# Attention and gate in one kernel: the value products in two row halves with a PSUM bank each, and six shared banks instead of seven

## The chip, the cores and the metric

The kernel runs on one core of a Trainium2 chip. The metric is the time of one execution on the device in microseconds. The core's engines work in parallel, each on its own queue of instructions: TensorE multiplies (PE in the profile; its weight loads are listed apart as PEld), VectorE (DVE) and ScalarE (ACT) do elementwise work and reductions, GpSimd (POOL) works between SBUF tiles, SyncE (SP) starts the transfers. Products land in PSUM, eight banks of 128 partitions by 512 f32, and are read from there by DVE and ACT.

## The reference

With `x` of 2048 rows and 640 columns, 32 heads of 20 columns and a hidden width of 1536 (`xn` is `x` normalised by row):

```python
q, k, v = split_heads(xn @ wqkv)
p = softmax(q @ k.T * 20 ** -0.5)            # for each head, 2048 x 2048
s = merge_heads(p @ v) @ wo
g = silu(relu(xn @ w1) @ w2)
out = x + s * g
```

The change touches `p @ v` and the division by the softmax's sum that follows it.

## The kernel before

Heads are worked on in 8 groups of 4 (`NG`), the queries in 4 chunks of 512 (`NC`, `CW`), the keys in 16 tiles of 128 (`NT`). One *step* is a group, a chunk and a key tile: 8 x 4 x 16 = 512 steps (`STEPS`).

For every group and chunk the kernel does three things with the scores:

- It finds the largest score of each query. `mx_unit` (lines 617 to 638) multiplies queries by keys in f16 into a PSUM bank (line 629), and DVE takes the maximum of the bank (line 633). `highest` and `rows` (lines 640 to 691) gather the maxima, turn them with one transpose into a PSUM bank (line 661), and send them into two extra rows of the packed queries.
- It computes the scores again the other way round, keys by queries, with the maximum subtracted by the extra rows. `st_unit` (lines 719 to 746) does the product (line 732), and ACT writes the exponentials in f32 into a tile `pt` (line 736). Four such products, one for each head, make the weights of one step; three `pt` tiles are in use in turn (`PTS`).
- It weighs the values. `weigh` (lines 764 to 776) multiplies, for each of the four heads, the 128 keys of the step (f32, 21 columns: 20 of the head and a one, which sums the weights) by the 512 weights, and adds the product into the bank `pv`. Head `h` writes partitions 32h to 32h + 20, so four products with a stationary operand of 128 rows and 21 columns stand side by side in the array. After 16 steps `normalise` (lines 780 to 819) copies `pv` into an SBUF tile `sb` of 128 x 512, by ACT or DVE, whichever the plan has free earlier (lines 783 to 788). Later `rest` turns `sb` with four transposes into one shared bank (line 794), and DVE divides (lines 797 and 800).

The score products have 60 or 62 rows. They are always issued in pairs (`pair`, lines 645 to 656), one on rows 0 to 63 of the array and one on rows 64 to 127, each into a bank of its own. `KINDS` (line 1227) lists what may be paired: two scores for the maximum, two for the exponentials, or one of each.

All other large products are *fill*: the projections of queries, keys and values, the gate's two layers and the output projection. `products` (lines 298 to 320) cuts each of them into row halves as well: two results, two banks, and each half of the 128 rows goes to one of the two tiles of 64 rows, first straight, then crossed (line 314). Without score work to go with it, `whole` (lines 322 to 330) uses all 128 rows (line 328). A fill product holds its two banks from its first matmul until ACT or DVE has read them.

PSUM holds `pv` (line 173) and 7 shared banks (`BANKS`, line 174). Scores, fill products and the transposes take shared banks with `take` (lines 182 to 187), which gives the one that comes free first; a pair or a fill product needs two (`take_two`, and `soonest(2)` in `choose`).

The order of all engines' instructions is made when the program is built, by a planner (`Plan`, lines 81 to 154) and a loop over it (lines 1252 to 1301). It keeps a clock for each engine and estimated costs in ns (lines 52 to 78: `PAIR` 220 for a pair, `PV` 850 for a step of values, `SWITCH` 100 between kinds of matmul, `EXP` 585, `RED` 605). At each turn it issues a pair if banks are free and ACT or DVE will soon run out of work; else one or two steps of values, if their weights are ready (`pv_count`, lines 748 to 762; the first step of a chunk also waits for `pv_free`, the time at which the copy of the last chunk is done); else small work such as the transposes; else a fill product, at a pace that spreads the fill over the attention (`pace`, lines 1245 to 1250). Each engine then runs its own queue in that order and waits on semaphores for what it reads or overwrites.

Of the kernel before, what the change touches and what calls it, by code (L numbers as in the profile page):

```python
# [11 lines left out]
F32 = mybir.dt.float32  # L12
# [5 lines left out]
P = 128  # L18
# [3 lines left out]
DH = 20  # L22
# [3 lines left out]
NT = S // P  # L26
CW = 512
# [5 lines left out]
NP = H // 2  # L33
RING = 4
PTS = 3
BANKS = 7
STEPS = NG * NC * NT
INF = float("inf")

# [118 lines left out]
def attention_gate(ctx: ExitStack, tc: tile.TileContext, x, wqkv, wo, w1, w2, out):  # L158
    nc = tc.nc
    ctx.enter_context(tc.manual_schedule())  # L160
    plan = Plan()
# [7 lines left out]
    psum = ctx.enter_context(tc.tile_pool(name="psum", bufs=1, space=bass.MemoryType.PSUM))  # L169

    pv = psum.tile([P, CW], F32, name="pv")
    banks = [psum.tile([P, CW], F32, name=f"ps{i}") for i in range(BANKS)]
    bank_free = [0.0] * BANKS
    behind = [0] * BANKS

# [4 lines left out]
    def take():  # L182

        i = min(range(BANKS), key=lambda i: bank_free[i])
        ready = bank_free[i]
        bank_free[i] = INF
        return i, ready
# [5 lines left out]
    nc.vector.memset(ones_row, 1.0)  # L193
    root = const.tile([1, 1], F32, name="root")
    nc.scalar.activation(root, ones_row[:, 0:1], AF.Sqrt)
    nc.vector.memset(pv, 0.0)

    qk_d = {w: dram.tile([D, 3, S], F16, name=f"{w}_d") for w in "qk"}
    h_d = {part: dram.tile([DFF, S], F16, name=f"h{part}_d") for part in "hl"}
# [23 lines left out]
    def soon(ready, cost, fn):  # L223
        small.append((ready, cost, fn))
# [329 lines left out]
    va = [vap.tile([P, NT, H // 2, DH + 1], F32, name=f"va{n}") for n in range(2)]  # L554
# [142 lines left out]
    pv_free = [0.0]  # L697
# [8 lines left out]
    def where(step):  # L706
        return step // (NC * NT), step // NT % NC, step % NT
# [56 lines left out]
    def weigh():  # L764
        step = pv_done[0]
        g, c, k = where(step)
        pv_done[0] += 1
        pt = pts.pop(step)
        plan.seen = max(plan.seen, st_issued.pop(step))
        got = plan.pe("P", PV, max(p_ready.pop(step), pv_free[0] if k == 0 else 0))  # L770
        for h in range(4):
            nc.tensor.matmul(pv[32 * h:32 * h + DH + 1, :], va[g // 4][:, k, 4 * (g % 4) + h, :], pt[:, h, :],  # L772
                             start=(k == 0), stop=(k == NT - 1))
        pt_free[step] = plan.t + BACK
        if k == NT - 1:
            normalise(g, c, got)
# [3 lines left out]
    def normalise(g, c, got):  # L780
        epool = pools["ep"]
        sb = epool.tile([P, CW], F32, name=f"pvs{g}{c}", tag="pvs")
        if plan.free["act"] < plan.free["dve"]:
            nc.scalar.copy(sb, pv)
            pv_free[0] = plan.op("act", 600, got)
        else:
            nc.vector.tensor_copy(sb, pv)
            pv_free[0] = plan.op("dve", 690, got)

        def rest():  # L790
            b, free = take()
            tp = banks[b].rearrange("p (i h d) -> p i h d", i=TPC, h=4)
            for i in range(TPC):
                nc.tensor.transpose(banks[b][:, i * P:(i + 1) * P], sb[:, i * P:(i + 1) * P], ident)
            got = plan.pe("F", 4 * TURN, free)
            rl = epool.tile([P, TPC, 4], F32, name=f"rl{g}{c}", tag="rl")
            nc.vector.reciprocal(rl, tp[:, :, :, DH])
            plan.op("dve", 250, got)
            dst = on if g + 1 < NG else on[:, :, P - 4 * DH:]
            nc.vector.tensor_mul(dst.rearrange("p i (h d) -> p i h d", d=DH), tp[:, :, :, 0:DH],  # L800
                                 rl[:, :, :, None].to_broadcast([P, TPC, 4, DH]))
            bank_free[b] = done = plan.op("dve", 490)
            if g + 1 < NG:
                def go():
                    rows = o_d[c * CW:(c + 1) * CW, :].rearrange("(i p) e -> p i e", p=P)
                    nc.sync.dma_start(rows[:, :, 4 * DH * g:4 * DH * (g + 1)], on)
                    o_stored[g, c] = plan.arrival(4 * P * 4 * 4 * DH)

                plan.at(done, go)
            else:  # L810
                first.append(out_rest(c, on, done))

        if g + 1 < NG:
            on = epool.tile([P, TPC, P], F32, name=f"on{g}{c}", tag="on", bufs=NC)[:, :, 0:4 * DH]
        else:
            on = epool.tile([P, TPC, P], F32, name=f"on{g}{c}", tag="on", bufs=NC)
            nc.sync.dma_start(on[:, :, 0:P - 4 * DH],
                              o_d[c * CW:(c + 1) * CW, KL * P:D - 4 * DH].rearrange("(i p) e -> p i e", p=P))
        soon(pv_free[0], 4 * TURN, rest)
# [235 lines left out]
    def out_rest(c, on, ready):  # L1055

        yield from when(lambda: pre_done[0] >= (c + 1) * TPC)
        tail, wot, cs_o, pre = (out_state[n] for n in ("tail", "wo", "scale", "pre"))
        gts = []
        for i in range(TPC):  # L1060
            t = c * TPC + i
            gts.append(tail.tile([P, D], F32, name=f"gr{t}", tag="gr", bufs=6))
            landed = load(gts[i], g_d[t * P:(t + 1) * P, :], 4 * P * D)
        o, ready = yield from transposed(f"r{c}", on, TPC, ready, "r")
        for i in range(TPC):
            t = c * TPC + i
            gt = gts[i]
            ot = o[0][:, i:i + 1, :], o[1][:, i:i + 1, :]
            ws = [w[:, KL:KD, :] for w in wot]
            bs, free = take_two()  # L1070
            got = yield from whole([banks[b][:, 0:HD] for b in bs],
                                      [terms(ot, ws, 1, slice(0, P), ns) for ns in halves], max(free, ready))
            for n, (b, ns) in enumerate(zip(bs, halves)):
                ps = banks[b][:, 0:HD]
                nc.vector.scalar_tensor_tensor(gt[:, ns], ps, cs_o, gt[:, ns], op0=ALU.mult, op1=ALU.mult)  # L1075
                bank_free[b] = done = plan.op("dve", 550, max(got, landed))
                if n and c + 1 == NC:
                    nc.vector.tensor_add(gt[:, ns], gt[:, ns], pre[:, t, ns])  # L1078
                    done = plan.op("dve", 500, done)
                else:  # L1080
                    nc.gpsimd.tensor_add(gt[:, ns], gt[:, ns], pre[:, t, ns])
                    done = plan.op("pool", 880, done)
            plan.at(done, lambda t=t, gt=gt: nc.sync.dma_start(out[t * P:(t + 1) * P, :], gt))
# [168 lines left out]
    while True:  # L1252
        plan.due()
        t = plan.t
# [11 lines left out]
        if n and (coming == INF or min(plan.free["act"], plan.free["dve"]) - t > STOCK or plan.mode != "A"):  # L1266
            for _ in range(n):
                weigh()
            log.append((t, f"pv{n}"))
            continue  # L1270
# [22 lines left out]
        if pv_done[0] * 4 + 4 <= st_done[0]:  # L1293
            g, c, k = where(pv_done[0])
# [32 lines left out]
```

## Time and profile before

| | |
|---|---|
| time, median of 2 runs | 1789.01 us (1787.75 to 1790.27) |
| the profiled execution: its time | 1788.3 us |
| the profiled execution: its span, first to last instruction | 1786.5 us |
| mean granted TensorE clock | 0.992 of full speed |
| idle PE waiting for GpSimd at the start (line 418, longest single wait of PE) | 14.3 us |
| normalise's copies | 23 on ACT, 9 on DVE |
| first and last value product | 125.7 and 1769.8 us |

The profile is one execution, recorded by the hardware. Its rows are groups of instructions: source line, engine, operation, what it writes and reads (buffer numbers left out, so `ps` is any of the shared banks), the shape, how many, then busy time in us, the mean duration of one in ns, and the time that the engine sat idle just before them, with what ended it. For a matmul the shape begins with the rows and columns of the stationary operand: 62*128 is 62 rows and 128 columns. An f32 matmul appears as two, one for each pass over its operand, so line 772 has 4096 rows in the trace for 2048 in the program. Matmuls are pipelined: one of 512 columns is listed with 378 ns while the next starts about 220 ns after it, so busy times of PE overlap and a busy PE is not a PE at its peak. In rows of the order of time the first two numbers are the start and the length in us, and x8 means that eight instructions of one kind follow each other there.

### The profile page before, as it was taken

The numbers are of one execution on the slowest core, as the hardware profiler recorded it, in microseconds if no ns is written. First come the engines' busy times: TensorE is split into PE (matmuls) and PEld (weight loads), VectorE is DVE, ScalarE is ACT, GpSimd is POOL, SyncE is SP. The second block draws the span as 40 slices with busy tenths as digits, with TensorE's granted clock in tenths as the row PEclk, the third lists the DMA queues.
The fourth block names the chain that finished last, engine by engine and source line by source line (L and its number), as shares of the span: only waits on it lengthen the run. The fifth ranks groups of instructions, "written<-read, shape, count | busy, mean of one in ns | idle before, by whom it ended". The sixth has DMA issues, their size and how long they took to land. (4 is left out here: it accounts for less than half of the span.)

```text
span 1786.5 us, 36686 instructions
## 1 busy us (share of the span) xinstructions
PE 1734.0 (97%) x14887; PEld 723.6 (41%) x14887; DVE 1451.6 (81%) x2512; ACT 1390.6 (78%) x2338; POOL 315.9 (18%) x338
## 2 busy tenths in 40 slices
PE   4999999999999999999999989999999999999998
PEld 3443334444332333444433324444444444344332
DVE  7699988888888888888888878888888888887522
ACT  3537788888888888887887868888788878887785
POOL 1631200002111455322221103000000000012221
PEclk8999999999999999999999999999999999999998
DMA  6324311201115332311112071131013100323332
GB/s 240 102 62 125 99 33 35 49 20 37 58 41 162 96 93 89 107 51 43 45 39 73 29 216 42 55 92 56 13 55 92 55 9 20 109 87 124 102 100 74
DMA packets 133995, 135.30 MB, mean 76 GB/s; under 512 B 26640, under 2 KB 110480, under 8 KB 133824
## 3 DMA queue, kind: packets, MB, share of 16 engines
q1 hardware_dynamic: 133248, 131.63, 24.4%
q8 instruction: 116, 1.90, 0.4%
q10 hardware_dynamic: 576, 1.31, 0.2%
q14 instruction: 55, 0.45, 0.1%
HBM read 85.32 MB, written 47.58 MB: 74 GB/s over the span
## 5 line engine op out<-in xcount | busy, mean ns | idle before, releaser
L736 ACT ACTIVATE pt<-ps,cexp 128x512 f32<-128x512 f32 x2048 | 1249.4, 689 | 293.0 <-PE ps L732 244.8
L633 DVE TENSOR_REDUCE m<-ps 128x1 f32<-128x512 f32 x2048 | 1274.4, 684 | 211.0 <-PE ps L629 204.6
L629 PE MATMUL ps<-kp,qp 60*128 60x512 f16 x2048 | 585.6, 378 | 5.3 <-ACT pt L736 3.7
L732 PE MATMUL ps<-qp,kp 62*128 62x512 f16 x2048 | 579.4, 379 | 9.3 <-DVE m L633 4.7
L772 PE MATMUL pv<-pt,va 128*21 128x512 f32 x4096 | 523.0, 600 | 0.0
L732 PEld LDWEIGHTS <-kp 62*128 62x128 f16 x2048 | 147.3, 93 | 332.2 <-issue 289.6
L629 PEld LDWEIGHTS <-qp 60*128 60x128 f16 x2048 | 150.1, 93 | 117.3 <-issue 84.7
L772 PEld LDWEIGHTS pv<-pt,va 128*21 128x21 f32 x4096 | 88.4, 100 | 237.3 <-issue 226.4
L1048 POOL TENSOR_TENSOR pre<-pre,go 128x320 f32<-128x320 f32 x32 | 27.0, 864 | 596.3 <-DVE go L1046 596.3
L314 PE MATMUL ps<-w2th,hh 64*128 64x320 f16 x768 | 126.5, 296 | 0.1
L314 PE MATMUL ps<-w2th,hl 64*128 64x320 f16 x768 | 126.0, 295 | 0.0
L314 PE MATMUL ps<-w2tl,hh 64*128 64x320 f16 x768 | 125.6, 295 | 0.0
L314 PEld LDWEIGHTS <-hh 64*128 64x128 f16 x1536 | 88.2, 94 | 51.2 <-issue 10.5
L314 PE MATMUL ps<-xt_hi,1h 64*128 64x512 f16 x480 | 102.7, 376 | 0.0
L314 PE MATMUL ps<-xt_lo,1h 64*128 64x512 f16 x480 | 102.1, 375 | 0.0
L314 PE MATMUL ps<-xt_hi,1l 64*128 64x512 f16 x480 | 100.3, 375 | 0.5 <-POOL 1l L287 0.5
L314 PEld LDWEIGHTS <-1h 64*128 64x128 f16 x960 | 58.7, 94 | 53.0 <-issue 18.7
L896 POOL CAST hh<-hr 128x512 f16<-128x512 f32 x48 | 29.3, 610 | 287.2 <-ACT hr L894 258.5
L482 POOL TENSOR_TENSOR loq<-rq,hiq 128x512 f16<-128x512 f32 x16 | 18.5, 1159 | 260.2 <-ACT rq L480 260.2
L314 PE MATMUL ps<-xt_hi,qh 64*128 64x512 f16 x150 | 56.4, 376 | 0.0
L314 PE MATMUL ps<-xt_lo,qh 64*128 64x512 f16 x150 | 56.4, 376 | 0.0
L898 POOL TENSOR_TENSOR hl<-hr,hh 128x512 f16<-128x512 f32 x48 | 55.7, 1160 | 3.8
(219 smaller groups left out, 1521.7 us busy)
## 6 DMA issues: line engine op xcount, KB each, us to landing
kp<-k_d SPq DMA_DIRECT2D x28, 240.0 KB
qp<-q_d SPq DMA_DIRECT2D x28, 240.0 KB
hh_d<-hh SPq DMA_DIRECT2D x48, 128.0 KB
hl_d<-hl SPq DMA_DIRECT2D x48, 128.0 KB
hh<-hh_d SPq DMA_DIRECT2D x8, 768.0 KB
hl<-hl_d SPq DMA_DIRECT2D x8, 768.0 KB
q_d<-hiq SPq DMA_DIRECT2D x20, 256.0 KB
k_d<-hik SPq DMA_DIRECT2D x20, 256.0 KB
```

The source lines that it names most:

```text
L314: nc.tensor.matmul(ps[which], a[rows], b[rows], start=(i == 0 and not second), stop=(i == n - 1 and bool(second)))
L482: nc.gpsimd.tensor_sub(lo, r, hi)
L629: nc.tensor.matmul(banks[b], qp[p % RING][r, t:t + P], kp[p % RING][r, kc * CW:(kc + 1) * CW], start=True, stop=True)
L633: nc.vector.tensor_reduce(m4[:, 2 * pr + j, qt, kc:kc + 1], banks[b], axis=AX.X, op=ALU.max)
L732: nc.tensor.matmul(banks[b], kp[p % RING][r, k * P:(k + 1) * P], qp[p % RING][r, c * CW:(c + 1) * CW], start=True, stop=True)
L736: exps[step, u] = nc.scalar.activation(pt[:, u, :], banks[b], AF.Exp, scale=cexp).ins
L772: nc.tensor.matmul(pv[32 * h:32 * h + DH + 1, :], va[g // 4][:, k, 4 * (g % 4) + h, :], pt[:, h, :], start=(k == 0), stop=(k == NT - 1))
L896: nc.gpsimd.tensor_copy(hi, r)
L898: nc.gpsimd.tensor_sub(lo, r, hi)
L1048: nc.gpsimd.tensor_add(pre[:, t, ns], pre[:, t, ns], gts[t][:, ns])
```

## The change

The values of a step are multiplied in two halves of 64 keys. There are two value banks, `pv[0]` for keys 0 to 63 of every tile and `pv[1]` for keys 64 to 127, so each head's product of 128 rows becomes two of 64 rows, both of 512 columns, with 21 columns of stationary operand as before. When a chunk is done, ACT copies the first bank into `sb` and DVE adds the second to it; there is no choice of engine any more, and `pv_free` is set after the add. With two of the eight PSUM banks for values, six are shared. The planner's costs for a step of values (`PV`) and its kinds of matmul stay as they are.

```diff
-BANKS = 7
+BANKS = 6
...
-    pv = psum.tile([P, CW], F32, name="pv")
+    pv = [psum.tile([P, CW], F32, name=f"pv{i}") for i in range(2)]
...
-    nc.vector.memset(pv, 0.0)
+    for t in pv:
+        nc.vector.memset(t, 0.0)
...
         got = plan.pe("P", PV, max(p_ready.pop(step), pv_free[0] if k == 0 else 0))
         for h in range(4):
-            nc.tensor.matmul(pv[32 * h:32 * h + DH + 1, :], va[g // 4][:, k, 4 * (g % 4) + h, :], pt[:, h, :],
-                             start=(k == 0), stop=(k == NT - 1))
+            for half in range(2):
+                rows = slice(half * P // 2, (half + 1) * P // 2)
+                nc.tensor.matmul(pv[half][32 * h:32 * h + DH + 1, :], va[g // 4][rows, k, 4 * (g % 4) + h, :],
+                                 pt[rows, h, :], start=(k == 0), stop=(k == NT - 1))
...
         sb = epool.tile([P, CW], F32, name=f"pvs{g}{c}", tag="pvs")
-        if plan.free["act"] < plan.free["dve"]:
-            nc.scalar.copy(sb, pv)
-            pv_free[0] = plan.op("act", 600, got)
-        else:
-            nc.vector.tensor_copy(sb, pv)
-            pv_free[0] = plan.op("dve", 690, got)
+        nc.scalar.copy(sb, pv[0])
+        done = plan.op("act", 600, got)
+        nc.vector.tensor_add(sb, sb, pv[1])
+        pv_free[0] = plan.op("dve", 690, done)
```

## The prediction

> **What bounds the kernel now.** I read the page's head first, then a table by stage, then the page's costliest groups, and last the order of time on TensorE around the values (line 772).
>
> ```profile
> span 1786.5 us, 36686 instructions
> PE 1734.0 (97%) x14887; PEld 723.6 (41%) x14887; DVE 1451.6 (81%) x2512; ACT 1390.6 (78%) x2338; POOL 315.9 (18%) x338
> ...
> 0.00:126.00 126.00, 100.76 (x574) 51.91 (x578) 97.09 (x208) 51.70 (x92) 43.97 (x49) 0.96 0.42 141
> 126.00:1750.00 1624.00, 1605.09 (x14147) 661.69 (x14143) 1343.54 (x2285) 1320.23 (x2217) 265.10 (x282) 1.00 0.24 71
> 1750.00:1786.00 36.00, 28.19 (x172) 10.04 (x172) 10.94 (x20) 18.69 (x32) 6.86 (x8) 0.87 0.11 42
> ```
>
> The columns of the table are stretch, length, then busy time of PE, PEld, DVE, ACT and POOL, the granted clock, DMA. In the long middle stage PE is busy 1605 of 1624 us at the full clock, DVE 83%, ACT 81%. So time is PE's: a change pays or costs what it takes off or puts on PE there, and the other two have some 280 and 300 us to give.
>
> ```profile
> L736 ACT ACTIVATE pt<-ps,cexp 128x512 f32<-128x512 f32 x2048 | 1249.4, 689 | 293.0 <-PE ps L732 244.8
> L633 DVE TENSOR_REDUCE m<-ps 128x1 f32<-128x512 f32 x2048 | 1274.4, 684 | 211.0 <-PE ps L629 204.6
> L629 PE MATMUL ps<-kp,qp 60*128 60x512 f16 x2048 | 585.6, 378 | 5.3 <-ACT pt L736 3.7
> L772 PE MATMUL pv<-pt,va 128*21 128x512 f32 x4096 | 523.0, 600 | 0.0
> ```
>
> But a busy PE is not a streaming PE. The values are the only large work that leaves the array's 64-row form (60*128, 62*128 and 64*128 in the rows, two tiles side by side) for another: 128*21, four heads side by side. What a visit to that form costs is in the order of time:
>
> ```profile
> 901.52 0.38 PE L314 MATMUL ps<-xt_hi,1l 64*128 64x512 f16 x2
> 901.74 0.38 PE L732 MATMUL ps<-qp,kp 62*128 62x512 f16 x2
> 902.05 1.06 PE L772 MATMUL pv<-pt,va 128*21 128x512 f32 x8
> 903.04 0.39 PE L629 MATMUL ps<-kp,qp 60*128 60x512 f16 x2
> ...
> 1131.77 1.92 PE L772 MATMUL pv<-pt,va 128*21 128x512 f32 x16
> 1133.61 0.39 PE L732 MATMUL ps<-qp,kp 62*128 62x512 f16 x2
> ```
>
> Pairs inside the 64-row form start 0.22 us apart (901.52 to 901.74). The last pair before the values holds the array 0.31 us, 0.09 more. One step of values (x8: each f32 product is two passes, for four heads) takes 0.99 us until the next pair starts, two steps (x16) 1.84. So a step more is 0.85, a pass 0.43, and 0.99 - 0.85 leaves about 0.13 per visit besides the streaming. With the 0.09 ahead, a visit has 0.22 us that is not streaming.
>
> ```profile
> 125.69 1.31 PE L772 MATMUL pv<-pt,va 128*21 128x512 f32 x8
> ...
> 1766.28 4.15 PE L772 MATMUL pv<-pt,va 128*21 128x512 f32 x16
> ```
>
> Between these two, the first and the last, I count 378 visits: 244 of x8 and 134 of x16 (244 + 268 = 512 steps). 378 x 0.22 = 83 us. That is all the change could win on PE, and the question is whether 64-row values (64*21) still leave the form of the scores (62*128).
>
> **The change part by part.**
>
> *Values in halves.* The nearest row is a place where only the width changes:
>
> ```profile
> 1689.99 0.30 PE L328 MATMUL ps<-wo_h,olr 128*128 128x320 f16 x1
> 1690.12 0.30 PE L328 MATMUL ps<-wo_h,ohr 128*128 128x320 f16 x1
> 1690.35 1.06 PE L772 MATMUL pv<-pt,va 128*21 128x512 f32 x8
> ```
>
> Here both sides use 128 rows. The L328 products run 0.13 to 0.14 us apart, the values come 0.23 after the last: 0.095 us lost, as much as the 0.09 where rows and width change together. Equal rows buy nothing as long as the width goes from 128 to 32. After the change rows are equal and the width still goes from 128 to 32, so I take the price of a visit's two ends as unchanged. Its bounds: all of both ends won (0.09 + 0.095 a visit, 70 us), or nothing; I take nothing, since the row with the same single difference says so. By the Trainium skill (TensorEngine Tiling (Array Packing), Key Properties) another tiling mode drains the array and another tile of the same mode does not; as it lists 64x128 and 64x32 apart, its sum would be the same, and the L328 row, where only the width changes, agrees with 0.095 us.
>
> Each step now issues 16 instead of 8 matmuls, and as many weight loads. A half needs as many columns as a whole (512), so a pass stays 0.43 us if all eight tiles run side by side. What grows is the staggered start:
>
> ```profile
> 902.04:902.05 0.01, 0.00 (x1) 1.00 0.00 0
> 902.05:902.06 0.01, 0.01 (x2) 1.00 0.00 0
> 902.06:902.07 0.01, 0.01 (x4) 1.00 0.00 0
> ```
>
> Counts of L772 in 10 ns stretches: one tile has begun in the first, four in the third, so three more starts take about 0.02 us, 0.007 each. Four more tiles: 0.027 us a visit, x 378 = 10 us, on the path, since the next pair needs the whole array. Bounds: 0 (stagger hidden in the 0.13) and, should the whole 0.13 less the 0.095 of the exit scale with the tiles, another 0.035, 13 us. I take 10, as it is counted. By the Trainium skill (TensorE: Matmul & The Clock Gate, Measured speedup vs the span model) one more tile costs about 4 ns; by that page the term would be an estimated 6 us and the sum 4 us lower; the 7 ns of this trace stand.
>
> *Normalise.* One copy, by whichever engine is freer, becomes ACT copy, then DVE add, 32 times.
>
> ```profile
> L784 ACT COPY pvs<-pv x23: 585/585/647, 172.3 to 1678.7; 128x512 f32<-128x512 f32 x23
> L787 DVE COPY pvs<-pv x9: 668/692/693, 287.0 to 1770.5; 128x512 f32<-128x512 f32 x9
> L196 DVE MEMSET pv<- x1: 485/485/485, 1.1 to 1.1; 128x512 f32 x1
> ...
>   PEld pv L772: 2.2, 7
> ```
>
> ACT gets 9 copies more (9 x 0.585 = 5 us); DVE gets 32 adds for 9 copies. No add of this shape is in the trace, I price it as the DVE copy, 0.69: 23 x 0.69 = 16 us. Both lie in the idle time named above. If that cover were gone, 16 us of DVE would be the price. The new wait: the add stands in DVE's queue until ACT's copy is done, so the reduces (L633) behind it wait, up to 32 x 0.59 = 19 us of DVE, and the banks those reduces free come later to PE; fill products (L314) stand in for that. And the two value banks come free 0.7 us later per chunk. Today PE lost 2.2 us to that release in 32 chunks. Bounds: 0, if the next chunk's values come later anyway, and 32 x 0.7 = 22 us if nothing else could run. I take 2, near the row.
>
> The last chunk has no cover:
>
> ```profile
> 1770.47 0.69 DVE L787 COPY pvs<-pv 128x512 f32<-128x512 f32 x1 [6.01 <-PE pv L772]
> 1771.22 0.66 PE L794 MATMUL ps<-ident,pvs 128*128 128x128 f32 x4 [0.79 <-DVE pvs L787]
> ```
>
> PE waits for this copy at the end of the kernel; copy and add in a row make it 0.59 longer: +0.6 us. The second memset (0.49 us at 1.1 us) is long done when the first values start at 125.69: nothing, at most 0.5.
>
> *Six shared banks.* A pair takes two, a running fill product two. 7 = fill + two pairs + one odd bank; 6 = fill + two pairs. What used the odd one are single-bank jobs and a pair that starts when the banks of another come free one by one.
>
> ```profile
> L661 PE MATMUL ps<-ident,m x32: 275/277/383, 112.0 to 1673.5; 128*16 128x128 f32 x32
> L794 PE MATMUL ps<-ident,pvs x128: 272/273/333, 173.3 to 1771.6; 128*128 128x128 f32 x128
> L1011 PE MATMUL ps<-ident,ot x64: 272/273/331, 1543.2 to 1742.2; 128*128 128x128 f32 x64
> L1011 PE MATMUL ps<-ident,on x16: 272/328/422, 1626.4 to 1773.4; 128*128 128x128 f32 x16
> ...
> PE ps L732 <- DVE m L633: 4.7, 7, 2.3
> PE ps L629 <- ACT pt L736: 3.7, 19, 0.3
> ```
>
> That is 32 + 128/4 + 80/4 = 84 jobs. Each now keeps a pair from being in flight, and ACT and DVE run dry for about one operation, 0.7 us (L736, L633): up to 84 x 0.7 = 59 us of theirs. PE's own waits for banks are some 8 us today (the two rows above), because a fill product or values fill the hole; the order is planned anew with six. Bounds for PE: 0 and 59; I take 5, near the waits of today. A new order can also have more or fewer visits, 0.22 us each; I have no row for that.
>
> *Sum.* 1788.3 us is the profiled execution's own time (its span of 1786.5 and 1.8 around it), 0.7 below the median of 1789.0. 1788.3 + 10 (stagger) + 2 (release of the value banks) + 0.6 (end) + 5 (banks) = 1806 us, 1.0% above the median.
>
> **The rivals.**
>
> *The ends of a visit vanish* (faster). If the array only empties when its row grouping changes, 64-row values follow 62-row scores as one pair follows another, and 378 x (0.09 + 0.095) = 70 us go: 1736 us. For it: pairs of 60, 62 and 64 rows follow each other without loss. Against: L328 to L772, the same rows and still 0.095 lost. The other engines would allow it (DVE busy 1452 + 16).
>
> *The halves do not run side by side* (slower). No row shows eight tiles at once. If the second half's first pass queues behind the first half's second, each visit lasts a pass longer: 378 x 0.43 = 163, 1969 us. If every step is doubled, 512 x 0.85 = 435, 2241 us. Against: two row tiles run at once in every pair (x2 lasts 0.38, one matmul 378 ns), and four column tiles in the values.
>
> *Six banks starve the scores* (slower). The price is the 59 us above; it decides where more than 23 of them meet no fill, since 1789 + 36 (2%) less the 13 of the other terms is there. The worst is 1788.3 + 12.6 + 59 = 1860. For it: fill holds two banks nearly always. Against: PE's waits for banks are small, and PE itself has fill to run until 1750.
>
> **How the numbers follow.** Forecast as summed, with its own range of 1785 (no cost of banks, no stagger, some visits fewer) to 1824: 0.62. Ends vanish, about 1736: 0.14. Halves not side by side, 1969 or more: 0.09. Banks starve, 1825 to 1860: 0.15. Two per cent, about what a measurement of this kernel can tell from no change, is 36 us, 1753 to 1825. So faster 0.14, same 0.62, slower 0.24. The range must leave out no more than 0.2: from 1732 (the ends vanish, with 4 us to spare) to 1850, which leaves out the serial halves and the worst of the banks.
>
> **What would show it.** In the order of time: from the last pair to the values still 0.31, and 1.01 to 1.03 from the first of sixteen matmuls to the next pair; 0.22 and 0.86 would be the ends vanishing, 1.4 the halves in a row. In the group rows: about 8192 value matmuls, 32 copies on ACT and 32 adds on DVE of 0.7 us. In the waits: PE's waits for L633 and L736 at a few us; tens would be the banks. The prediction is wrong if PE's loss at a visit differs from 0.22 + 0.03, or if PE idles over 40 us in the middle stage.

## The result, and the profile after

The changed kernel takes 1959.72 us (median of 2 runs, 1959.01 to 1960.44) against 1789.01 before: a ratio of 1.0954, 95% interval 1.0928 to 1.0980. That is 171 us more, outside the forecast range.

The page of the changed kernel, head and groups, and one row of the table by stage (stretch, length, busy time of PE, PEld, DVE, ACT and POOL, clock, DMA); line numbers are one to three higher than before:

```profile
span 1958.7 us, 44976 instructions
PE 1870.2 (95%) x18977; PEld 776.4 (40%) x18977; DVE 1472.3 (75%) x2535; ACT 1403.3 (72%) x2348; POOL 315.4 (16%) x338
...
L737 ACT ACTIVATE pt<-ps,cexp 128x512 f32<-128x512 f32 x2048 | 1255.2, 694 | 437.9 <-PE ps L733 390.4
L634 DVE TENSOR_REDUCE m<-ps 128x1 f32<-128x512 f32 x2048 | 1280.3, 684 | 334.5 <-PE ps L630 326.6
L775 PE MATMUL pv<-pt,va 64*21 64x512 f32 x8192 | 548.3, 598 | 2.4 <-ACT pvs L786 2.4
...
126.00:1923.00 1797.00, 1743.97 (x18221) 715.95 (x18221) 1374.80 (x2328) 1331.86 (x2223) 266.54 (x284) 0.99 0.22 65
```

The scores' readers do the same work in the same time each (694 and 684 ns against 689 and 684), but ACT now stands idle 437.9 us ahead of the exponentials instead of 293.0, and DVE 334.5 ahead of the maxima instead of 211.0, nearly all of it until PE delivers scores. And PE still looks 97% busy in the middle stage. All three engines wait for each other. One sign of being wrong that the forecast named has come up: PE idles 53 us in the middle stage (1797.00 less 1743.97), where it named 40.

The values did what the forecast said. In the order of time of the changed kernel (start, length):

```profile
906.01 0.38 PE L630 MATMUL ps<-kp,qp 60*128 60x512 f16 x2
906.32 1.08 PE L775 MATMUL pv<-pt,va 64*21 64x512 f32 x16
907.34 0.39 PE L733 MATMUL ps<-qp,kp 62*128 62x512 f16 x1
...
912.17 1.94 PE L775 MATMUL pv<-pt,va 64*21 64x512 f32 x32
914.05 0.39 PE L733 MATMUL ps<-qp,kp 62*128 62x512 f16 x2
```

The entry is 0.31 us as before, a visit of one step 1.02 instead of 0.99, of two steps 1.88 instead of 1.84. The ends of a visit have not vanished, and the eight tiles do run side by side. I add up, from the start of each matmul to the start of the next, by its form, in us (the 128-row form: stationary operands of 128*128 and 128*16):

```
                          64-row form   values   128-row form   visits of values
before                         1106.0    498.5          152.7                378
changed                        1247.9    525.6          154.7                358
six banks alone (below)        1248.0    515.2          156.6                364
```

Of the 171 us more in these columns, 142 lie in the 64-row form: the scores and the fill, whose arithmetic the change did not touch. They are the same products; what has grown is the time between them. Of the 27 us more in the values' column six banks with whole values have 17 as well, so most of that is not the price of the halves. One place in the changed kernel:

```profile
899.74 3.01 ACT L737 ACTIVATE pt<-ps,cexp 128x512 f32<-128x512 f32 x5
899.89 3.07 DVE L634 TENSOR_REDUCE m<-ps 128x1 f32<-128x512 f32 x5
...
900.48 0.37 PE L733 MATMUL ps<-qp,kp 62*128 62x512 f16 x1
900.62 0.37 PE L630 MATMUL ps<-kp,qp 60*128 60x512 f16 x1
900.70 0.52 PE L315 MATMUL ps<-xt_hi,1l 64*128 64x512 f16 x2
901.06 0.37 PE L733 MATMUL ps<-qp,kp 62*128 62x512 f16 x1
901.22 0.37 PE L630 MATMUL ps<-kp,qp 60*128 60x512 f16 x1
901.27 0.54 PE L315 MATMUL ps<-xt_hi,1h 64*128 64x512 f16 x2
```

A score pair and a fill pair, which need 0.22 us each, now take 0.58 (900.48 to 901.06). The two matmuls of a pair start 0.14 us apart instead of together. Each is listed with 0.37 us, so the gaps between starts don't show as idle time: the share of busy time hides the wait. The semaphores in the trace tell what it is: each of the four scores here starts 0.04 us after one that its own reader has set, ACT for L733 and DVE for L630. So PE waits for a bank at each of them. At this place the readers run without a pause (five exponentials in 3.01 us, five maxima in 3.07) and set the pace; what they lost, they lost where they stood idle.

Two rivals were on the table for a time like this. The halves in a row would have given 1969 us, close to what was measured, but would show visits of 1.4 us, and the median visit of one step takes 1.013. The other was the banks.

### The profile page after: what moved, and what is told of

It reads as the page before. It is cut to its first block, busy times and chain, and to the rows that moved or that the text cites. A ratio compares the mean times of both kernels' runs of the same rounds, so it can differ in the third digit from the quotient of the medians.

```text
span 1958.7 us, 44976 instructions
## 1 busy us (share of the span) xinstructions
PE 1870.2 (95%) x18977; PEld 776.4 (40%) x18977; DVE 1472.3 (75%) x2535; ACT 1403.3 (72%) x2348; POOL 315.4 (16%) x338
## 4 chain that ended last, share of the span: by engine, by line
PE 80%; ACT 12%; DVE 4%; DMA 2%; issue 1%; SPq 1%; POOL 0%; DVEq 0%; ACTq 0%
PE pv L775 24%; PE ps L315 22%; PE ps L733 17%; PE ps L630 11%; ACT pt L737 11%; PE ps L329 2%; DVE m L634 2%; PE ps L501 1%; PE ps L795 1%; DMA op<-in_A_wo 1%; DMA 2p<-in_B_w 1%; SPq L209 1%; PE ps L1012 1%; PE ps L662 0%; DVE st L367 0%
## 5 line engine op out<-in xcount | busy, mean ns | idle before, releaser
L737 ACT ACTIVATE pt<-ps,cexp 128x512 f32<-128x512 f32 x2048 | 1255.2, 694 | 437.9 <-PE ps L733 390.4
L634 DVE TENSOR_REDUCE m<-ps 128x1 f32<-128x512 f32 x2048 | 1280.3, 684 | 334.5 <-PE ps L630 326.6
L733 PE MATMUL ps<-qp,kp 62*128 62x512 f16 x2048 | 597.3, 379 | 24.7 <-ACT pt L737 9.9
L630 PE MATMUL ps<-kp,qp 60*128 60x512 f16 x2048 | 612.5, 377 | 8.2 <-DVE m L634 4.2
L775 PE MATMUL pv<-pt,va 64*21 64x512 f32 x8192 | 548.3, 598 | 2.4 <-ACT pvs L786 2.4
L733 PEld LDWEIGHTS <-kp 62*128 62x128 f16 x2048 | 152.6, 93 | 383.7 <-issue 306.0
L630 PEld LDWEIGHTS <-qp 60*128 60x128 f16 x2048 | 161.8, 93 | 197.7 <-issue 147.7
L775 PEld LDWEIGHTS pv<-pt,va 64*21 64x21 f32 x8192 | 111.1, 96 | 250.0 <-issue 223.3
L315 PE MATMUL ps<-w2th,hl 64*128 64x320 f16 x768 | 141.2, 296 | 1.1 <-DMA hl<-hl_d 1.1
L315 PE MATMUL ps<-w2tl,hh 64*128 64x320 f16 x768 | 140.9, 296 | 0.0
L315 PE MATMUL ps<-w2th,hh 64*128 64x320 f16 x768 | 139.8, 296 | 0.0
L788 DVE TENSOR_TENSOR pvs<-pvs,pv 128x512 f32<-128x512 f32 x32 | 22.0, 688 | 83.0 <-ACT pvs L786 80.9
L315 PEld LDWEIGHTS <-hl 64*128 64x128 f16 x768 | 50.2, 94 | 19.2 <-issue 4.3
```

The source lines that it names most:

```text
L315: nc.tensor.matmul(ps[which], a[rows], b[rows], start=(i == 0 and not second), stop=(i == n - 1 and bool(second)))
L630: nc.tensor.matmul(banks[b], qp[p % RING][r, t:t + P], kp[p % RING][r, kc * CW:(kc + 1) * CW], start=True, stop=True)
L634: nc.vector.tensor_reduce(m4[:, 2 * pr + j, qt, kc:kc + 1], banks[b], axis=AX.X, op=ALU.max)
L733: nc.tensor.matmul(banks[b], kp[p % RING][r, k * P:(k + 1) * P], qp[p % RING][r, c * CW:(c + 1) * CW], start=True, stop=True)
L737: exps[step, u] = nc.scalar.activation(pt[:, u, :], banks[b], AF.Exp, scale=cexp).ins
L775: nc.tensor.matmul(pv[half][32 * h:32 * h + DH + 1, :], va[g // 4][rows, k, 4 * (g % 4) + h, :], pt[rows, h, :], start=(k == 0), stop=(k = ...
```

## The experiments

All are compared with the kernel before on the same chip. Theory B says that six shared banks cost the time, V that the halved values do, N that the later release of the value banks does.

**Six banks alone.** One line of the kernel before:

```diff
-BANKS = 7
+BANKS = 6
```

> The kernel before with BANKS = 6 and nothing else. Theory B (the shared banks: with six, the score pairs wait for banks and the planned order itself gets longer): 1930 to 1975 us, PE time between value visits as long as in the changed kernel. Rival V (the halved values cost it: more matmuls, a bank collision, another form of the array): 1780 to 1800, since values are whole here. Rival N (the later release of the value banks after copy and add): 1780 to 1800 as well.

Measured: 1951.26 us, ratio 1.0907 (1.0891 to 1.0924). That is 162 of the 171 us, with whole values, one value bank and the old copy. The granted clock, 0.991 to 0.995, is that of the kernel before. The groups of its page show much the same idle times as the changed kernel, and its order of time shows one way in which the banks bind:

```profile
L736 ACT ACTIVATE pt<-ps,cexp 128x512 f32<-128x512 f32 x2048 | 1257.0, 695 | 430.4 <-PE ps L732 367.3
L633 DVE TENSOR_REDUCE m<-ps 128x1 f32<-128x512 f32 x2048 | 1284.1, 684 | 365.2 <-PE ps L629 355.9
...
800.62 0.47 PE L629 MATMUL ps<-kp,qp 60*128 60x512 f16 x2
...
801.27 0.47 PE L732 MATMUL ps<-qp,kp 62*128 62x512 f16 x2
...
802.23 0.61 PE L629 MATMUL ps<-kp,qp 60*128 60x512 f16 x2
...
803.00 0.49 PE L732 MATMUL ps<-qp,kp 62*128 62x512 f16 x2
...
803.43 0.38 PE L629 MATMUL ps<-kp,qp 60*128 60x512 f16 x1
803.98 0.37 PE L629 MATMUL ps<-kp,qp 60*128 60x512 f16 x1 [0.18 <-DVE m L633]
```

Here both scores of a pair go to one engine, which frees their banks one after the other. A pair for DVE (L629) follows the last one after 1.61 us, a pair for ACT (L732) after 1.73. The round of two banks is about 0.4 us of matmul and two reads in a row, some 1.8 us: DVE ends its second read of the pair of 800.62 at 802.41. The first matmul of the next pair starts shortly before that, and the second follows when its bank is free (x2 lasts 0.61 there instead of 0.38; in the last two rows the wait for DVE is long enough to be listed). ACT's two reads of the pair of 801.27 last from 801.68 to 802.95, and ACT then stands for 0.58 us. With fill on two banks and such a pair on each two of the other four, no pair can start until two banks are nearly free. Somewhat over half of this run's pairs are of this kind; in the others each engine reads one bank.

**The copy and the add alone.** Seven banks, whole values; the same bank is added once more, so sums and weights are both doubled and their quotient stays:

```diff
-        if plan.free["act"] < plan.free["dve"]:
-            nc.scalar.copy(sb, pv)
-            pv_free[0] = plan.op("act", 600, got)
-        else:
-            nc.vector.tensor_copy(sb, pv)
-            pv_free[0] = plan.op("dve", 690, got)
+        nc.scalar.copy(sb, pv)
+        done = plan.op("act", 600, got)
+        nc.vector.tensor_add(sb, sb, pv)
+        pv_free[0] = plan.op("dve", 690, done)
```

> The kernel before with seven banks and whole values, but every chunk is copied by ACT and then added to by DVE (the same bank is added once more, so sums and weights are both doubled and their quotient stays). Theory B: 1788 to 1805 us. Rival V: the same. Rival N: 1880 or more.

Measured: 1795.92 us, 1.0036 (1.0021 to 1.0050): 4 to 9 us. N falls as the cause.

**The halves alone.** Seven banks, one value bank, only the first half of each tile's keys:

```diff
-            nc.tensor.matmul(pv[32 * h:32 * h + DH + 1, :], va[g // 4][:, k, 4 * (g % 4) + h, :], pt[:, h, :],
-                             start=(k == 0), stop=(k == NT - 1))
+            rows = slice(0, P // 2)
+            nc.tensor.matmul(pv[32 * h:32 * h + DH + 1, :], va[g // 4][rows, k, 4 * (g % 4) + h, :],
+                             pt[rows, h, :], start=(k == 0), stop=(k == NT - 1))
```

> The kernel before with seven shared banks and one value bank, with values of 64 rows: only keys 0 to 63 of each tile are multiplied, the products of keys 64 to 127 are left out. Theory B: the form of 64 rows and 21 columns costs nothing by itself and wins nothing at the ends of a visit: 1783 to 1795 us, 0.31 us from the last pair to the values and 0.99 to the next pair. Rival V: over 1830, or visits that take 1.4 us. If the ends of a visit vanished with equal rows: about 1720.

The products of the other 64 keys are left out. Measured: 1792.84 us, 1.0028 (1.0018 to 1.0039). Its order of time:

```profile
904.03 0.38 PE L732 MATMUL ps<-qp,kp 62*128 62x512 f16 x2
904.35 1.05 PE L773 MATMUL pv<-pt,va 64*21 64x512 f32 x8
905.34 0.39 PE L629 MATMUL ps<-kp,qp 60*128 60x512 f16 x2
```

Entry 0.32, visit 0.99: a stationary operand of 64 rows and 21 columns costs at its ends what one of 128 rows and 21 columns does. With that, and with six banks alone at 162 of the 171 us, V falls, and so does the hope that equal rows would save the ends. What the run does not hold is the second half with its bank; its price is seen only in the visits of the changed kernel.

**Five banks alone**, to see how the cost grows:

```diff
-BANKS = 7
+BANKS = 5
```

> The kernel before with BANKS = 5 and nothing else. Theory B: each bank less costs as much again or more, since fill keeps its two: 2110 to 2250 us. If only the one odd bank matters and banks count in pairs (four left for scores as good as five, three as good as two): either no more than 1965, or a jump that six had not shown.

Measured: 2244.44 us, 1.2546 (1.2521 to 1.2571). One bank less costs 162 us, the next 293 more. The granted clock was lower there too, which may be some of it (with six banks it was 0.995):

```profile
core 0: 2243.6 us, clock 0.933
```

Counted in pairs, seven and six would have been alike, with two pairs in flight beside the fill. They are not: each single bank counts.

**Mixed pairs.** The changed kernel, where the planner prefers a pair of one score for ACT and one for DVE; both engines then read at the same time and the two banks come free together:

```diff
-MIXED = 400
+MIXED = 2000
```

> The changed kernel with MIXED = 2000 instead of 400, so that the planner prefers pairs of one score for ACT and one for DVE, whose two banks come free together, to pairs whose banks one engine frees one after the other. Theory B, with this as the way in which the banks bind: 1840 to 1890 us. If banks bind only through the fill products that hold them, or if V or N holds: 1945 to 1970, no change.

Measured: 1889.51 us, 1.0565 (1.0549 to 1.0580). 70 of the 171 us come back without a bank more. In its trace 454 score pairs have their two matmuls start more than 0.06 us apart, against 980 in the changed kernel and 647 in the kernel before (of some 2045 each). The same line in the kernel before, with its seven banks:

> The kernel before, seven banks, with MIXED = 2000 as in the changed kernel with mixed pairs. Theory B: with a spare bank it matters little in what order banks come free: 1775 to 1800 us. If mixed pairs are better by themselves, whatever the banks: 1690 to 1750.

Measured: 1791.07 us, 1.0009 (0.9999 to 1.0019). With the odd bank it doesn't matter in what order banks come free; without it, it is worth 70 us.

**Mixed pairs and no pace.** The changed kernel with `MIXED = 2000` and

```diff
-            return AHEAD + FILLING * (1 + n / ((NG - 1) * NC * NT))
+            return INF
```

> The changed kernel with mixed pairs, and pace() without a bound, so that fill products may run whenever they are ready. Theory B with fill held back by the pace while scores wait for banks, so that PE stands between them: 1855 to 1880 us. If PE's loss in the scores does not come from fill held back: 1885 to 1895, no change.

Measured: 1874.08 us, 1.0476 (1.0460 to 1.0492): 15 us more come back. Fill held back is a small part. This is the fastest version with six banks that I ran, and still 85 us behind the kernel before.

**Asking early.** In the changed kernel the planner places a pair 400 ns before it reckons two banks to be free; PE waits on the semaphores for the rest (`EAGER = 400`):

```diff
-        two = soonest(2)
+        two = soonest(2) - EAGER
...
-        got = plan.pe("A", PAIR, max(at, free))
+        got = plan.pe("A", PAIR, max(at, free - EAGER))
```

> The changed kernel, in which the planner puts a score pair into the order 400 ns before the time at which it reckons two banks to be free; the semaphores still hold PE back until they are. If the loss with six banks is the planner's caution (banks are free on the chip, the order comes late): 1790 to 1850 us. If the banks are truly short: PE stands at the head of its queue in place of a planned gap, fill can't pass the waiting pair, 1940 to 2050, and PE's waits for ACT and DVE in the profile grow from some 15 us to over 100.

Measured: 2003.87 us, 1.1197 (1.1179 to 1.1216). The time is in the range for banks truly short, but not for the reason given there. The rows are: PE's largest sum of listed waits on a score's bank, the value products with first and last start, and the fill in the 128-row form after 1860 us.

```profile
PE ps L734 <- ACT pt L738: 37.5, 138, 0.8
...
L776 PE MATMUL pv<-pt,va x8192: 589/589/1057, 132.1 to 1889.6; 64*21 64x512 f32 x200
...
1860.00:2001.00 141.00, 84.24 (x552) 54.45 (x552) 0.94 0.53 185
```

PE's listed waits for score banks stay well under 100 us, and counted by starts and semaphores, as under *Rows in order*, its waits for them come to an estimated 193 us against 175 in the changed kernel. The attention is done earlier, its last values at 1889.6 instead of 1942.0 us. But scores that ask early take the banks from the fill, which also needs two, and 84 us of it are left in the 128-row form for the end. With mixed pairs and no pace the time is above both ranges as well as above the 1874 us without asking early:

> The changed kernel with mixed pairs and no pace, with pairs put into the order 400 ns early as well. Caution of the planner: under 1830 us. Banks truly short: 1860 to 1950, no better than the 1874 without it.

Measured: 1994.48 us, 1.1148 (1.1131 to 1.1165). And in the kernel before, with `EAGER = 200`:

> The kernel before, seven banks, with pairs put into the order 200 ns early. A control for the two runs above: if asking early is worth something whatever the banks, 1740 to 1775 us; if a wait at the head of PE's queue costs more than a planned gap, 1795 to 1850.

Measured: 1856.04 us, 1.0371 (1.0355 to 1.0386), just over the upper range. Asking early is bad with seven banks too, so these three runs do not decide how much of the loss is the planner's caution. What they show is that scores and fill draw on one stock of banks: what the one gets sooner the other gets later.

**Rows in order.** The out-of-step starts of 0.14 us suggested another theory: that swapping which half of the array goes first makes one tile wait for the other. In the kernel before:

```diff
-                for which in range(2):
+                for which in (second, 1 - second):
                     rows = half[which ^ second]
...
-        for b, (mm, _) in zip(bs, two):
+        for b, (mm, _, _) in sorted(zip(bs, two), key=lambda e: e[1][2]):
             mm(b)
```

(the third entry is the half, `j`.)

> The kernel before, seven banks, the same planned order, but in every pair and in every fill product the matmul on rows 0 to 63 is issued first (in the kernel before the order is swapped from one pair to the next and in the second half of a product). If the two tiles fall out of step because a matmul that is issued second has its weights loaded only after the first one has begun, and the swap makes it the leading tile that then waits: 1700 to 1770 us. If tiles are out of step only because a bank came late: 1785 to 1795, no change.

Measured: 1795.15 us, 1.0036 (1.0023 to 1.0049). No gain: the theory fell. That one of the two banks comes late is shown by the semaphores in the traces. In the changed kernel 980 of 2041 score pairs start more than 0.06 us out of step; in 909 of them the second matmul starts within 0.08 us after a semaphore that an exponential or a maximum has set, mostly 0.04 us after it. Of the 783 pairs in step, with at most 0.02 us between them, 46 do. Being out of step is not the cost by itself: in the run with rows in order only 331 pairs are, and it is no faster.

The same count gives the size of the wait. I take each score in the 64-row form that starts so soon after its reader's semaphore, by how much it is behind the pitch of 0.22 us, and halve the sum, since two tiles run side by side. That is an estimated 65 us in the kernel before, 175 in the changed one and 170 with six banks alone. So about 110 of the 142 us more in the 64-row form are PE standing for banks in its own queue.

## Why the prediction was wrong

The step that failed is the term for the six shared banks: 5 us taken, bounds 0 and 59, and 162 measured by changing nothing but that. The mechanism was there as a rival, "six banks starve the scores", with a chance of 0.15 and a worst case of 1860; its price was off, and with it the range.

The mistake is in the sentence that 7 is fill, two pairs and one odd bank, and that the odd one serves 84 single-bank jobs. I counted banks in pairs, and the jobs that use one. But banks do not come free in pairs. The odd bank serves any of the 4096 scores: as soon as one bank of a pair is read, it and the odd one carry the next pair. I had the rows for the reads, 2048 of 689 ns and 2048 of 684: a pair for one engine holds its second bank for the matmul and two reads, some 1.8 us, and with two such pairs in flight, one for each engine, no bank is left to put the matmul of the next pair beside the reads of this one. The price was to be sought with 4096 scores, not with 84 transposes.

The second mistake is the cover. I wrote that PE fills its holes with fill. Fill takes two banks from the same stock, and PE's waits of some 8 us, near which I took the term, were no measure. The view counts a wait only from the listed end of the matmul before, which is 0.38 us after its start, while the next could start after 0.22; shorter waits don't appear in it. By starts and semaphores PE stood an estimated 65 us for banks in the kernel before, behind the 8 that I read.

The other steps:

- *The ends of a visit stay.* Right: entry 0.31 us in the changed kernel. The halves alone gave a ratio of 1.0028 (1.0018 to 1.0039) instead of winning 70 us.
- *The stagger of four more tiles.* Right: the median of all one-step visits, start of the values to start of the next pair, is 1.013 us against 0.990, so 0.023 against the 0.027 forecast. With 358 visits instead of 378 part of it was given back.
- *The copy and the add.* 2.6 us forecast, 6.8 measured alone. I bounded DVE's wait for the copy by 32 x 0.59 = 19 us, and the view of the changed kernel lists four times that. Who waited for the value tiles there (us, times):

```profile
  DVE pvs L788: 80.9, 27
  ACT pvs L786: 27.7, 22
  PEld pv L775: 5.2, 6
```

But 61.5 of DVE's 80.9 us are three waits in the last three chunks (10.3, 26.1 and 25.0), when DVE had little left to do; the other 24 sum to 19.4, at the bound. ACT's copy mostly did not queue: ACT stood idle for PE's last values ahead of 22 of the 32 copies. PE listed 2.4 us of waits for a copy, and the run by itself costs 6.8.
- *The end.* Copy 0.58 and add 0.69 us stand in a row in the last chunk, as forecast.

Put together, banks 162, copy and add 7, halves 4 make 173 us beside the 171 measured. That it fits so closely is partly luck: the run with the halves leaves out the second half, and so the stagger, 358 x 0.023 or an estimated 8 us. The changed kernel is 8.5 us above six banks alone: that is what the halves, the second value bank and the add cost when the banks are gone already.

What stays open: mixed pairs and no pace bring back 85 of the 171 us; how the other 85 split between pairs that need two banks at once and fill that holds two was not separated. The traces say where the readers stand idle. From 126 us to the last values ACT does so for 305 us before and 460 in the changed kernel. Of the 155 us more, 86 lie in gaps that touch a visit of values or the 0.7 us after one, in which PE makes no score and readers have only the banks filled ahead, and 70 elsewhere. Mixed pairs win back 27 of the 86 and 43 of the 70; with no pace as well, 29 and 31 are left. That six banks also leave too few filled ahead of a visit is argued from this count, and no run separates it. No run beat the kernel before.

## What to carry to other kernels

A buffer that one stage takes from a shared pool is missed by everything that draws on the pool, and the first sum to make is that of the round trips: number of users times the time each holds a buffer, over the number of buffers. It is only a lower bound. If every pair were for one engine, 4096 scores held for 1.1 or 1.8 us would take an estimated 1485 us of the four banks beside fill, less than the 1624 of the middle stage, and yet going from seven banks to six cost 162. What users that need two banks at once add to it had to be measured. Engines that wait for each other in a circle are a sign of a pool too small, even where no wait is long and the bound engine reads 95% busy; there the starts and the semaphores have to be counted. And a time that fits a rival is not yet the rival: the serial halves would have given the measured time within 10 us, and the visits of 1.02 us in the trace ruled them out.

## What the runs showed of the hardware

That the two tiles of the 64-row form drift apart was new to me: in the changed kernel 980 of 2041 score pairs start more than 0.06 us out of step (647 of 2044 before). Where they are 0.14 us apart, a score pair and a fill pair take 0.58 us instead of 0.44, and the busy share still reads 95%. That eight f32 tiles of 64 rows and 21 columns run side by side no row had shown before; they do, at 1.02 us for sixteen matmuls against 0.99 for eight. And equal row halves do not lower the price at the ends of a visit: from a score pair of 60 or 62 rows to values of 64 the entry is 0.31 to 0.32 us, as it is to values of 128.
